# A decode block of attention and feed-forward: 549 matrix products in place of 693

## The chip, the core and the metric

The kernel runs on one core of a Trainium2 chip. The metric is the device time of one execution in microseconds (us). The kernel before takes 236.25 us, the median of three runs (236.07 to 236.47). Everything is fp32. Instructions run on five engines, each in its own program order: PE (matrix products; PEld is its weight loads), DVE (vector), ACT (scalar), POOL and SP, which here only issues the transfers from device memory. Engines wait for one another through semaphores.

## The reference, cut to what matters

One token for each of two batch entries passes an attention block over the last 4096 keys of a cache, and then a feed-forward block:

```python
mod = (silu(c) @ w_mod).reshape(2, 6, 1, 512)          # sa, ca, ga, sb, cb, gb
h = layernorm(x) * (1 + ca) + sa
q = (h @ wq)                                            # 32 heads of 128, 8 key/value heads
p = softmax(q k^T * 128**-0.5)                          # over the last W = 4096 keys
x = x + ga * ((p v) @ wo)
h = layernorm(x) * (1 + cb) + sb
x = x + gb * (silu(h @ w1) @ w2)                        # 512 -> 1792 -> 512
```

The cache slices are 4 MB for each key/value head, batch entry and side (keys or values), sixteen heads and entries in all: 67 MB. With the weights it is 97.5 MB, and every byte of it is used once.

## The kernel before, in words

**Storage.** One SBUF buffer, `store`, has three slots of 64 KB per partition. Each slot holds either a whole cache piece (four key/value heads of one batch entry, keys or values, 8.4 MB) or weights. At the start slot 1 holds `w_mod` and small early tiles, slot 2 `wq`. The pieces then take the slots in turn in the order k0, k1, v0, k2, v1, k3, v2, v3 (`order`, slot `i % 3`), and after them `wo` goes to slot 2, and `w1` and `w2` to slot 0. All these transfers are issued by SP in this order, on one queue; SP waits before each until the slot's last reader is done. A transfer that waits holds back every later one. `fetch` at the end of each step of the loop only records them; what a transfer waits for are the readers of its slot: k2 the products of `turn(0)`, v1 those of `turn(1)`, k3 those of `values(0)`, v2 those of `turn(2)`, v3 those of `values(1)`, `wo` those of `turn(3)`, `w1` those of `values(2)`.

**Order.** There is no scheduler. `Flow.record` notes each operation with the earlier ones whose regions it overlaps, and `emit` writes the instructions of each engine in exactly the order of the program text, with a wait for each such operation on another engine. So the text of the loop sets what stands behind what on PE and on ACT. In a profile nearly all instructions have line L117, in `emit`, and are told apart by their tiles.

**A step of the loop**, t = 0 to 3, has four parts:

- `scores(t)`: eight DVE transposes of 128 x 2048 keys in place, and after each one four products (one for each key/value head, 16 rows of the result, 512 columns) into `bank_a`. Then the maximum, which passes through two small products (`sel`, `negscale`) and becomes a bias, and one `Exp` on ACT, which writes the probabilities into the first 1024 columns of the key slot and their sums into `rowsum`.
- `turn(t)`: one DVE transpose of these 1024 columns and 16 products with `sel` into `tp` (bank C), each with 128 columns: four positions n of a key within a group, by four key/value heads a.
- `spread(t)`: four ACT copies from `tp` into `ptb`, each with another mask of `par`, so that `ptb` has 16 columns (four key/value heads by four query heads) for each of 128 keys of a partition.
- `values(t)`: 64 products. Product i takes the 32 columns of `ptb` of two keys as weights and 256 columns of the value slot (two keys by 128) and adds into 32 rows of `o_ps`, rows 32 * (i % 4). Then ACT copies `o_ps` out (`ob`, into the slot's first columns), and two products with `pick` add up the two keys and the four row groups into `o_all`.

The text of the loop before:

```python
for t in range(NP):
    scores(t)
    if t > 1:
        values(t - 1)
    turn(t)
    if t == 1:
        values(0)
    spread(t)
    fetch(2 * t + 4)
values(NP - 1)
```

**After the loop.** `o_all` is divided by the sums on DVE, meanwhile PE has six products of idle work (`fill`, 512 columns with 128 columns of weights, results unused). Then the product with `wo`: 24 rows wide (`product`, 512 columns, four row groups by `q % 4`), copied out by ACT as `wide`; eight rows narrow (`narrow`: four products of 128 columns, one for each row group), and `wide` added by four products with `id4`. Then the second layer norm with small DVE operations, the product with `w1` in two halves (`hp[0]`, `hp[1]`, 16 products of 224 columns each), silu of each half, and the product with `w2`: 14 rows, all narrow, into `y`. The first seven rows need the first half's silu, the other seven the second half's. Two DVE operations and a transfer to device memory end the kernel.

Of the kernel before, what the change touches and what calls it, by code (L numbers as in the profile page):

```python
# [5 lines left out]
AF = mybir.ActivationFunctionType  # L6
ALU = mybir.AluOpType
# [6 lines left out]
U = 4  # L14
# [121 lines left out]
def adaln_block(nc, x, k_cache, v_cache, wq, wo, w1, w2, c, w_mod, out):  # L136
# [54 lines left out]
    def const(shape, name):  # L191
        return buf(name, *shape)
# [33 lines left out]
    def summed(shape, name, pattern, axis=AX.X, **sizes):  # L226
# [26 lines left out]
        ident.rearrange("p (u n i) -> p n i u", u=U, n=4),  # L253
    )
    par = summed([P, U], "par", "p (y u) -> p u y", u=U)

    pick = const([P, 2, U * G, 4], "pick")
    dve.tensor_reduce(
        pick[:, :, :, 0],
        ident.rearrange("p (c n w) -> p n w c", n=2, w=U * G),  # L260
        axis=AX.X,
# [9 lines left out]
    dve.memset(eps_t, EPS)  # L271
    mrow = const([1, P], "mrow")
    pool.memset(mrow, 0.0)
    qbd = const([P, 2, 4, B, 4, 16], "qbd")
# [117 lines left out]


    o_all = bank("O")[:, : B * DH].rearrange("p (b d) -> p b d", b=B)

    def scores(t):
        hh, b = seq[t]
        kv = kt[t].rearrange("p (n j r) -> p n j r", n=NK, j=4)
        for f in range(2):
            for j in range(4):  # L400
# [3 lines left out]
                for u in range(U):  # L404
# [6 lines left out]
                    )  # L411
        mx = buf(f"mx{t}", P, 1)
        dve.tensor_reduce(mx, bank_a, axis=AX.X, op=ALU.max)
# [13 lines left out]
        pe.matmul(bp[:, 0:1], mrow, negscale, start=True, stop=True)  # L427
        bias = buf(f"bias{t}", P, 1)
        act.copy(bias, bp[:, 0:1])
# [6 lines left out]
    def turn(t):  # L436
        pr = kt[t][:, :1024]
        dve.transpose(pr, pr)
        xp = pr.rearrange("p (f k w) -> p f k w", f=2, w=32)
        for n in range(4):  # L440
            for a in range(4):
                pe.matmul(
                    tp[32 * a : 32 * a + 32].rearrange(
                        "p (f k n g) -> p f k n g", f=2, n=4, g=G
                    )[:, :, :, n],
                    sel[:, 32 * n : 32 * n + 32],
                    xp[:, :, :, G * a : G * a + G],
                    start=True,
                    stop=True,
                    skip_group_check=True,  # L450
                )

    def spread(t):
# [5 lines left out]

    def values(t):  # L460
        hh, b = seq[t]
        o_ps = bank("D")
        for i in range(64):
            c_ = i % 4
            pe.matmul(
                o_ps[32 * c_ : 32 * c_ + 32, :256],
                ptb[:, 2 * i : 2 * i + 2, :].rearrange("p n w -> p (n w)"),
                vt[t][:, 256 * i : 256 * i + 256],
                start=(i < 4),
                stop=(i >= 60),  # L470
            )
        ob = vt[t][:, :256].rearrange("p (n d) -> p n d", n=2)
        act.copy(ob.rearrange("p n d -> p (n d)"), o_ps[:, :256])
        for n in range(2):
            pe.matmul(
                o_all[64 * hh : 64 * hh + 64, b],
                pick[:, n].rearrange("p w i -> p (w i)"),
                ob[:, n],
                start=(n == 0),
                stop=(n == 1),  # L480
                skip_group_check=True,
            )
# [18 lines left out]
    for t in range(NP):  # L501
        scores(t)

        if t > 1:
            values(t - 1)
        turn(t)
        if t == 1:
            values(0)
        spread(t)
        fetch(2 * t + 4)  # L510
    values(NP - 1)

# [70 lines left out]
    ao = bank("A")[:, :P]  # L583
    for i in range(6):
        fill(512)
# [50 lines left out]
    for h in range(2):  # L636
# [12 lines left out]
        dve.tensor_mul(uT[:, ts, 0:32:16], z[:, ts, :], sg)  # L649
    y = bank("D")[:, :P]  # L650
    for tt in range(T2):
        narrow(y, uT[:, tt, :], w2t[tt], tt == 0, tt == T2 - 1)
    yo = later(P)
# [30 lines left out]
```

## Time and profile before

| What | Value |
|---|---|
| median of three runs | 236.25 us (236.07 to 236.47) |
| the profiled execution's own time | 236.48 us |
| its span, from the first to the last instruction | 234.9 us |
| PE busy, products | 152.5 us, 1386 records (each fp32 product is two) |
| DVE busy | 103.4 us, 126 instructions |
| ACT busy | 26.6 us, 49 instructions |
| bytes moved, mean rate | 97.72 MB, 416 GB/s |

The profile is of one execution, and its times count from its first instruction. A row of a timeline gives the start and the duration in us, the engine, the operation, the tiles written and read with their shapes, the count, and in brackets how long the engine sat idle before it and what released it. A row of a table of windows gives the stretch, its length, each engine's busy time and count, the clock that PE was granted (1.00 is full, 0.50 half), the mean share of the 16 transfer engines that was busy, and GB/s; these shares are rough in short windows, since one packet is up to 64 KB. `SPq` is the issue of a transfer; the time from issue to landing is listed by the page.

### The profile page before, as it was taken

What the parts mean: (1) busy time and instruction counts of PE and PEld (TensorE: products, weight loads), DVE (VectorE), ACT (ScalarE), POOL (GpSimd) and SP (SyncE); (2) the same over time, 40 slices, a digit from 0 to 9 for tenths busy, and PEclk for the clock granted to TensorE, in tenths of its full rate; (3) what the DMA queues carried; (4) which work ended last, traced back from release to release, by engine and by line L of the source; (5) the groups of instructions that cost most, each with busy time, mean ns of one, the idle gap of its engine ahead of it and who ended that gap; (6) DMA issues with size and microseconds to landing.
All of it is one profiled execution on the core that took longest, in us unless ns stands there. A gap on an engine that the chain in (4) does not pass through costs nothing.

```text
span 234.9 us, 3022 instructions
## 1 busy us (share of the span) xinstructions
PE 152.5 (65%) x1386; PEld 49.3 (21%) x1386; DVE 103.4 (44%) x126; ACT 26.6 (11%) x49; POOL 6.6 (3%) x23
## 2 busy tenths in 40 slices
PE   0003906920699479965989969329979609998695
PEld 0002201210000020004510025200005405534254
DVE  5014130130999299942199840069962100200332
ACT  2003010010000240002050020500002220003200
POOL 5000000000000000000000000000000300000000
PEclk9999975875699859997999979956999967999769
DMA  7998998989899898989999999999999999999990
GB/s 268 444 528 368 435 457 357 527 357 526 368 446 446 368 505 379 513 379 424 449 391 483 402 480 391 416 457 413 449 435 457 393 427 418 421 406 435 414 370 33
DMA packets 2496, 97.72 MB, mean 416 GB/s; under 512 B 284, under 2 KB 308, under 8 KB 564
## 3 DMA queue, kind: packets, MB, share of 16 engines
q1 hardware_dynamic: 2460, 97.52, 96.7%
q8 instruction: 11, 0.18, 0.3%
q10 hardware_dynamic: 24, 0.01, 0.0%
q14 instruction: 1, 0.01, 0.0%
HBM read 97.53 MB, written 0.00 MB: 415 GB/s over the span
## 4 chain that ended last, share of the span: by engine, by line
DMA 46%; DVE 28%; PE 18%; another core or an unknown queue 3%; ACT 2%; issue 1%; SPq 0%; POOL 0%
DVE store L117 26%; DMA store<-in_A_wq_dram 15%; DMA store<-in_A_k_cache_dram 15%; DMA store<-in_B_w_dram 15%; PE bankD L117 11%; PE bankA L117 4%; PE bankC L117 2%; DVE mx L117 2%; ACT store L117 2%; PE bankB L117 1%; PE bankO L117 1%; SPq L117 0%; DVE qbd L117 0%; DVE mg L117 0%
## 5 line engine op out<-in xcount | busy, mean ns | idle before, releaser
L117 DVE STREAM_TRANSPOSE store<-store 128x2048 f32<-128x2048 f32 (+2 forms) x40 | 77.1, 1984 | 36.5 <-DMA store<-in_A_k_cache_dram 28.7
L117 PE MATMUL bankA<-store,qbd 128*16 128x512 f32 x256 | 64.7, 1081 | 23.0 <-DVE store L117 21.7
L117 PE MATMUL bankD<-store,ptb 128*32 128x256 f32 x512 | 31.6, 410 | 7.2 <-DMA store<-in_A_v_cache_dram 7.2
L117 PE MATMUL bankD<-store 128*32 128x512 f32 (+1 forms) x256 | 22.3, 502 | 8.8 <-DMA store<-in_A_wq_dram 8.3
L117 PE MATMUL bankB<-store 128*32 128x256 f32 (+3 forms) x72 | 7.8, 504 | 21.9 <-DVE store L117 21.9
L117 PEld LDWEIGHTS bankD<-store,ptb 128*32 128x32 f32 x512 | 17.3, 119 | 20.2 <-issue 10.7
L117 PEld LDWEIGHTS bankA<-store,qbd 128*16 128x16 f32 x256 | 4.3, 97 | 77.1 <-DVE store L117 77.1
L117 PEld LDWEIGHTS bankD<-store 128*32 128x32 f32 x256 | 8.2, 119 | 22.8 <-issue 21.5
L117 ACT ACTIVATE ptb<-bankC,par 128x512 f32<-128x512 f32 x16 | 11.0, 688 | 7.3 <-PE bankC L117 6.9
L117 ACT COPY bias<-bankB 128x1 f32<-128x1 f32 x4 | 0.6, 159 | 90.1 <-PE bankB L117 90.1
L117 PE MATMUL bankC<-store,sel 128*32 128x128 f32 x128 | 6.0, 348 | 5.5 <-DVE store L117 5.5
L117 PEld LDWEIGHTS bankB<-store 128*32 128x32 f32 (+1 forms) x72 | 4.2, 166 | 25.0 <-DVE store L117 22.6
L117 PE MATMUL bankC<-qbd,store 128*128 128x512 f32 (+1 forms) x18 | 9.0, 640 | 0.0
L117 DVE STREAM_TRANSPOSE store<-bankA 128x128 f32<-128x128 f32 (+1 forms) x2 | 0.7, 367 | 18.1 <-PE bankA L117 18.1
L117 DVE TENSOR_REDUCE mx<-bankA 128x1 f32<-128x1024 f32 x4 | 4.9, 1225 | 8.5 <-PE bankA L117 8.5
L117 DVE RECIPROCAL store<-bankB 128x2 f32<-128x2 f32 x1 | 0.2, 171 | 17.7 <-PE bankB L117 17.7
L117 ACT COPY store<-bankD 128x256 f32<-128x256 f32 (+1 forms) x6 | 2.5, 412 | 47.8 <-PE bankD L117 47.8
L117 DVE STREAM_TRANSPOSE store<-bankD 128x512 f32<-128x512 f32 x2 | 1.4, 719 | 12.1 <-PE bankD L117 12.1
L117 PE MATMUL bankA<-store 128*32 128x128 f32 (+1 forms) x96 | 5.2, 376 | 1.7 <-DMA store<-in_B_w_dram 0.9
L117 POOL MEMSET store<- 128x128 f32 (+2 forms) x7 | 2.4, 350 | 135.5 <-PE bankD L117 134.9
L117 PEld LDWEIGHTS bankC<-store,sel 128*32 128x32 f32 x128 | 4.4, 139 | 6.2 <-DVE store L117 5.7
L117 ACT ACT_TABLE_LOAD x4 | 5.1, 1283 | 2.8 <-DVE id L117 2.8
(76 smaller groups left out, 51.8 us busy)
## 6 DMA issues: line engine op xcount, KB each, us to landing
store<-in_w_mod_dram SPq DMA_DIRECT2D x1, 6144.0 KB, 17.3
store<-in_A_wo_dram SPq DMA_DIRECT2D x1, 6144.0 KB, 21.6
store<-in_B_w_dram SPq DMA_DIRECT2D x1, 3584.0 KB, 35.6
store<-in_A_wo_dram SPq DMA_DIRECT2D x1, 2048.0 KB, 27.7
store<-in_B_w_dram SPq DMA_DIRECT2D x1, 2048.0 KB, 40.1
store<-in_B_w_dram SPq DMA_DIRECT2D x1, 1024.0 KB, 42.0
store<-in_B_w_dram SPq DMA_DIRECT2D x2, 256.0 KB, 42.2
store<-in_A_k_cache_dram SPq DMA_DIRECT2D x4, 33.5
```

The costliest lines, as they stand in the source:

```text
L117: ins = getattr(eng, method)(*args, **kw)
```

## The change

Four things change, and some small tiles with them.

1. `turn` no longer makes 16 products with `sel`. Four masked copies of the transposed probabilities (512 elements a partition each, mask `key[:, n]`, two on DVE and two on ACT) are written to columns 1024 to 3071 of the key slot (`zp`), and four products of 512 columns with a new 32-column matrix `gather`, one for each head a, do the rest.
2. `values` has a parameter `wide`: the first `wide` keys go four to a product (64 columns of `ptb`, 512 columns of values, into 64 rows of `o_ps`), the others two to a product as before. It is 64 of 128 keys for t = 0, 2 and 3, all 128 for t = 1. The copy out of `o_ps` has 512 columns for 256, and four products with `pick` follow for two.
3. In the loop's step t = 2, `values(1)` now stands behind `turn(2)`; before, it stood ahead of it. `values(2)` keeps its place ahead of `turn(3)`.
4. The first eight rows of `w2` go wide (eight products of 512 columns for 32 of 128), are copied out by ACT into `wide` and added by four products with `id4`, behind rows 8 to 11 and ahead of rows 12 and 13. Of the six products of idle work ahead of `wo`, two are left.

The small tiles: `key` and `gather` are made at the start (two more DVE reductions), `pick` is twice as large, `mx` and `bias` are one tile each for all steps, and `mrow` lies in the key slot, where POOL clears it in each step.

```diff
+    key = summed([P, 4], "key", "p (u n i) -> p n u i", axis=AX.XY, u=U, n=4)
+    gather = const([P, 32], "gather")
+    dve.tensor_reduce(
+        gather.rearrange("p (i u) -> p i u", u=U),
+        ident.rearrange("p (u n i) -> p i u n", u=U, n=4),
+        axis=AX.X,
+        op=ALU.add,
...
-    pick = const([P, 2, U * G, 4], "pick")
+    pick = const([P, 4, U * G, 4], "pick")
...
-        ident.rearrange("p (c n w) -> p n w c", n=2, w=U * G),
+        ident.rearrange("p (c n w) -> p n w c", n=4, w=U * G),
...
+    mx, bias = const([P, 1], "mx"), const([P, 1], "bias")
...
-        mx = buf(f"mx{t}", P, 1)
+        mrow = kt[t][0:1, 3072:3200]
+        pool.memset(mrow, 0.0)
...
         xp = pr.rearrange("p (f k w) -> p f k w", f=2, w=32)
+        zp = kt[t][:, 1024:3072].rearrange("p (f k n w) -> p f k n w", f=2, n=4, w=16)
         for n in range(4):
-            for a in range(4):
-                pe.matmul(
-                    tp[32 * a : 32 * a + 32].rearrange(
-                        "p (f k n g) -> p f k n g", f=2, n=4, g=G
-                    )[:, :, :, n],
-                    sel[:, 32 * n : 32 * n + 32],
-                    xp[:, :, :, G * a : G * a + G],
-                    start=True,
-                    stop=True,
-                    skip_group_check=True,
+            if n < 2:
+                dve.tensor_scalar(
+                    zp[:, :, :, n], xp[:, :, :, :16], key[:, n : n + 1], None, op0=ALU.mult
                 )
+            else:
+                act.activation(
+                    zp[:, :, :, n], xp[:, :, :, :16], AF.Copy, scale=key[:, n : n + 1]
+                )
+        for a in range(4):
+            pe.matmul(
+                tp[32 * a : 32 * a + 32],
+                gather,
+                zp.rearrange("p f k n w -> p (f k n) w")[:, :, G * a : G * a + G],
+                start=True,
+                stop=True,
+            )
...
-    def values(t):
+    def values(t, wide):
+
         hh, b = seq[t]
         o_ps = bank("D")
-        for i in range(64):
-            c_ = i % 4
+        n0 = 0
+        while n0 < NK:
+            n = 4 if n0 < wide else 2
+            c = n0 // n % (8 // n)
+            r, d0 = 16 * n * c, n0 % 4 * DH
             pe.matmul(
-                o_ps[32 * c_ : 32 * c_ + 32, :256],
-                ptb[:, 2 * i : 2 * i + 2, :].rearrange("p n w -> p (n w)"),
-                vt[t][:, 256 * i : 256 * i + 256],
-                start=(i < 4),
-                stop=(i >= 60),
+                o_ps[r : r + 16 * n, d0 : d0 + n * DH],
+                ptb[:, n0 : n0 + n, :].rearrange("p n w -> p (n w)"),
+                vt[t][:, DH * n0 : DH * (n0 + n)],
+                start=(n0 < 8),
+                stop=(n0 + 8 >= NK),
+                skip_group_check=True,
             )
-        ob = vt[t][:, :256].rearrange("p (n d) -> p n d", n=2)
-        act.copy(ob.rearrange("p n d -> p (n d)"), o_ps[:, :256])
-        for n in range(2):
+            n0 += n
+        ob = vt[t][:, :512].rearrange("p (n d) -> p n d", n=4)
+        act.copy(ob.rearrange("p n d -> p (n d)"), o_ps)
+        for n in range(4):
             pe.matmul(
                 o_all[64 * hh : 64 * hh + 64, b],
                 pick[:, n].rearrange("p w i -> p (w i)"),
                 ob[:, n],
                 start=(n == 0),
-                stop=(n == 1),
+                stop=(n == 3),
                 skip_group_check=True,
...
-        if t > 1:
-            values(t - 1)
+        if t == 3:
+            values(2, 64)
         turn(t)
         if t == 1:
-            values(0)
+            values(0, 64)
+        if t == 2:
+            values(1, NK)
         spread(t)
         fetch(2 * t + 4)
-    values(NP - 1)
+    values(NP - 1, 64)
...
-    for i in range(6):
+    for i in range(2):
         fill(512)
...
-    y = bank("D")[:, :P]
-    for tt in range(T2):
-        narrow(y, uT[:, tt, :], w2t[tt], tt == 0, tt == T2 - 1)
+    y = bank("A")[:, :P]
+    acc = bank("D")
+    for tt in range(8):
+        product(acc, uT[:, tt, :], w2t[tt], tt % 4, D, tt < 4, tt >= 4)
+    act.copy(wide, acc)
+    for tt in range(8, T2 - 2):
+        narrow(y, uT[:, tt, :], w2t[tt], tt == 8, False)
+    narrow(y, id4, wide, False, False)
+    for tt in range(T2 - 2, T2):
+        narrow(y, uT[:, tt, :], w2t[tt], False, tt == T2 - 1)
```

Three places show how the instructions move. The first is PE in step t = 2, from its score products (into bank A) on; bank D with `ptb` is `values(1)`, bank O its sum over keys, bank C `turn(2)`. Shapes are rows by columns of the result. A minus is the order before, a plus the order now.

```order
 L117 MATMUL bankA<-store,qbd 16x512 x32
 L117 MATMUL bankB<-sel,mx 1x128
-L117 MATMUL bankB<-negscale,mrow 128x1
-L117 MATMUL bankD<-store,ptb 32x256 x64
-L117 MATMUL bankO<-store,pick 64x128 x2
-L117 MATMUL bankC<-store,sel 32x32x4 x16
+L117 MATMUL bankB<-negscale,store 128x1
+L117 MATMUL bankC<-store,gather 32x512 x4
+L117 MATMUL bankD<-store,ptb 64x512 x32
+L117 MATMUL bankO<-store,pick 64x128 x4
```

Before, `values(1)` ran while ACT and DVE made and transposed the probabilities of step 2, and `turn(2)` followed it. Now PE has `turn(2)` next after the two small products, and `values(1)` behind it, directly ahead of the score products of step 3.

The second is ACT in step t = 3, from the copy of the bias to the last copy out of `o_ps`:

```order
 L117 COPY bias<-bankB 128x1
 L117 ACTIVATE store,rowsum<-bankA,bias 128x1024
-L117 COPY store<-bankD 128x256
+L117 COPY store<-bankD 128x512
+L117 ACTIVATE store<-store,key 128x32x16 x2
 L117 ACTIVATE ptb<-bankC,par 128x128x4 x4
-L117 COPY store<-bankD 128x256
-L117 COPY store<-bankD 128x512
+L117 COPY store<-bankD 128x512 x2
 L117 ACT_TABLE_LOAD
```

The first copy from bank D is that of `values(2)`. The two masked copies of `turn(3)` stand behind it on ACT, and the products of `turn(3)` need them.

The third is the end of PE's program, the two halves of the product with `w1` (bank A, bank B) and the product with `w2`:

```order
 L117 MATMUL bankA<-store 32x224 x16
 L117 MATMUL bankB<-store 32x224 x16
-L117 MATMUL bankD<-store 32x128 x56
+L117 MATMUL bankD<-store 32x512 x8
+L117 MATMUL bankA<-store 32x128 x16
+L117 MATMUL bankA<-store,id 32x128 x4
+L117 MATMUL bankA<-store 32x128 x8
```

Seven of the eight wide products need the first half alone; the eighth and all that follows it need the second half too.

More of the change, by code (lines that the diff above doesn't have):

```diff
@@ L271, in adaln_block @@
     dve.memset(eps_t, EPS)
-    mrow = const([1, P], "mrow")
-    pool.memset(mrow, 0.0)
     qbd = const([P, 2, 4, B, 4, 16], "qbd")
@@ L427, in scores @@
         pe.matmul(bp[:, 0:1], mrow, negscale, start=True, stop=True)
-        bias = buf(f"bias{t}", P, 1)
         act.copy(bias, bp[:, 0:1])
@@ L439, in turn @@
         xp = pr.rearrange("p (f k w) -> p f k w", f=2, w=32)
+        zp = kt[t][:, 1024:3072].rearrange("p (f k n w) -> p f k n w", f=2, n=4, w=16)
         for n in range(4):
-            for a in range(4):
-                pe.matmul(
-                    tp[32 * a : 32 * a + 32].rearrange(
-                        "p (f k n g) -> p f k n g", f=2, n=4, g=G
-                    )[:, :, :, n],
-                    sel[:, 32 * n : 32 * n + 32],
-                    xp[:, :, :, G * a : G * a + G],
-                    start=True,
-                    stop=True,
-                    skip_group_check=True,
-                )
+            if n < 2:
+                dve.tensor_scalar(
+                    zp[:, :, :, n], xp[:, :, :, :16], key[:, n : n + 1], None, op0=ALU.mult
+                )
+            else:
[9 more added lines that the diff above has]
+                stop=True,
+            )
     def spread(t):
```

## The prediction, written before the changed kernel was run

> **What bounds the kernel now.** I read the page first, then the waits, then the timeline of the transfer queue beside that of PE.
>
> ```profile
> PE 152.5 (65%) x1386; PEld 49.3 (21%) x1386; DVE 103.4 (44%) x126; ACT 26.6 (11%) x49; POOL 6.6 (3%) x23
> DMA packets 2496, 97.72 MB, mean 416 GB/s; under 512 B 284, under 2 KB 308, under 8 KB 564
> q1 hardware_dynamic: 2460, 97.52, 96.7%
> q8 instruction: 11, 0.18, 0.3%
> ...
> store<-in_A_wo_dram SPq DMA_DIRECT2D x1, 2048.0 KB, 27.7
> ```
>
> The transfers are the bound: the queue is busy for 96.7% of the span, and PE only for 65%. So compute costs nothing as long as SP finds the next slot free before the transfer in flight has landed. How much room there is, the last cache pieces show:
>
> ```profile
> 0.74 0.39 SPq L117 DMA_DIRECT2D store<-in_w_mod_dram  x1
> 149.55 1.18 SPq L117 DMA_DIRECT2D store<-in_A_v_cache_dram  x2
> 155.02 17.66 DVE L117 STREAM_TRANSPOSE store<-store 128x2048 f32<-128x2048 f32 x8 [13.53 <-DMA store<-in_A_k_cache_dram]
> 186.67 0.81 SPq L117 DMA_DIRECT2D store<-in_A_wo_dram  x2
> 193.83 6.43 PE L117 MATMUL bankD<-store,ptb 128*32 128x256 f32 x92 [7.22 <-DMA store<-in_A_v_cache_dram]
> ...
> 1.50:2.00 0.50, 0.00 (x0) 0.00 (x0) 0.47 (x2) 0.00 (x0) 0.00 (x0) 1.00 4.06 1180
> ```
>
> k3 lands at 155.0, and v2 and v3 were issued at 149.55. v3 lands at 193.8, and `wo` was issued at 186.67, when `turn(3)` freed its slot: 7.1 us ahead. The first transfer was issued at 0.74 and its bytes moved from the half microsecond after 1.5 on, so an issue needs about 1.0 us. **The room is therefore 6.1 us for `turn(3)`**; after that the transfers stop. PE waits 7.22 us for v3.
>
> **PE's price of the new products.** A product is two records.
>
> ```profile
> 177.29 7.11 PE L117 MATMUL bankD<-store,ptb 128*32 128x256 f32 x128
> 203.33 5.42 PE L117 MATMUL bankC<-qbd,store 128*128 128x512 f32 x12
> 208.68 5.36 PE L117 MATMUL bankD<-store 128*32 128x512 f32 x48
> 202.69 0.32 PE L117 MATMUL bankO<-store,pick 128*64 128x128 f32 x1 [0.49 <-ACT store L117]
> 202.70 0.28 PE L117 MATMUL bankB<-rowsum,store 128*64 128x2 f32 x2
> 202.85 0.49 PE L117 MATMUL bankO<-store,pick 128*64 128x128 f32 x3
> 138.71 8.62 PE L117 MATMUL bankD<-store,ptb 128*32 128x256 f32 x128
> ...
> 138.70:142.00 3.30, 3.30 (x37) 0.53 0.82 357
> ```
>
> Six full-width products of 512 columns take 5.42 us, of which about 0.25 is the tail of the last: 0.86 each. Twenty-four products of 32 rows and 512 columns take 5.36: 0.86 for each round of four, so four row groups run side by side, and a round lasts by its columns alone. Sixteen rounds of 256 columns take 7.11, or 0.43 each. A product of 64 rows fills two row groups, and the 64-row products of `rowsum` (lower half) begin at 202.70 beside those of `pick` (upper half, 202.69), ahead of the latter's next ones at 202.85: two halves run side by side. So eight keys, which took one round of 256 columns (0.43), now take one of 512 (0.86). **`values` goes from 7.1 to 10.5 us where half is wide (+3.4), and to 13.9 where all is (+6.8).** Fewer products, but more columns per key. The bounds: as cheap as now (7.1), or no two halves side by side (17.3 and 27.5). `values(1)` took 8.62, with a granted clock of 0.53 in its first 3.3 us: such a start costs 1.5.
>
> The transfers' own term: 549 products are 2196 instructions of PE for 2772 (the page's 1386 + 1386). 0.18 MB of instructions came in 11 packets, about 252 instructions each, so nine remain. Such a packet delays data on one of the 16 transfer engines: the second piece of `wo` (2.1 MB, 5.0 us at 416 GB/s) landed 27.7 us after 187.1, at 214.8, though the first (21.6 us after its issue) was there at 208.3; 1.5 us are lost. I take 0 to 1.5 us earlier landings at the end, worth something only if the transfers set the end.
>
> **`turn`.** Removed: 16 products of 128 columns, four abreast, so as many columns as one round of 512. Added: one such round, 0.86 + 0.2, so the 1.08 us below stay. New on the path between the transpose and the products are the masked copies.
>
> ```profile
> 185.53 1.08 PE L117 MATMUL bankC<-store,sel 128*32 128x128 f32 x32
> 186.68 2.85 ACT L117 ACTIVATE ptb<-bankC,par 128x512 f32<-128x512 f32 x4 [1.78 <-PE bankC L117]
> ...
> L117 ACT ACTIVATE store<-store 128x14 f32<-128x14 f32 x2 | 0.4, 214 | 8.3 <-DVE store L117 8.3
> L117 DVE TENSOR_SCALAR store<-store 128x128 f32<-128x128 f32 x2 | 0.5, 228 | 0.5 <-ACT store L117 0.5
> ```
>
> ACT does 512 elements with a mask from PSUM in 0.71 (four in 2.85); from SBUF no row has 512, and 14 elements take 0.21. Two copies are between 0.43 and 1.43; I take 1.3, near the row of the same size. DVE's two lie beside them: between 0.46 (two of 128 elements) and 1.8 (four times that); I take 1.0. They also push back the transposes of the next keys by 1.0, which counts once, in step 1, where DVE has no wait ahead of them.
>
> **The backlog of scores.** This decides how far PE can catch up.
>
> ```profile
> 134.03 1.98 PE L117 MATMUL bankA<-store,qbd 128*16 128x512 f32 x8 [0.21 <-DVE store L117]
> ...
> 134.80:134.90 0.10, 0.10 (x4) 1.00 3.04 1311
> 134.90:135.00 0.10, 0.10 (x8) 1.00 0.00 0
> ...
> 135.10:135.20 0.10, 0.10 (x8) 1.00 1.52 655
> 135.20:135.30 0.10, 0.10 (x4) 1.00 0.00 0
> ```
>
> A group of four score products takes 1.98 us. Its second records begin near 134.9 while the first are still listed until 135.2. Groups that follow without a wait can overlap likewise: about 1.75 each, with 1.98 as the other bound. DVE sends a group every 2.2 us (17.66 / 8), so eight groups catch up 3.6 us at most.
>
> **The walk.**
>
> ```profile
> 110.16 7.54 PE L117 MATMUL bankD<-store,ptb 128*32 128x256 f32 x128
> 118.21 0.65 PE L117 MATMUL bankO<-store,pick 128*64 128x128 f32 x4 [0.50 <-ACT store L117]
> 136.08 1.23 DVE L117 TENSOR_REDUCE mx<-bankA 128x1 f32<-128x1024 f32 x1 [2.10 <-PE bankA L117]
> 140.25 1.25 DVE L117 STREAM_TRANSPOSE store<-store 128x1024 f32<-128x1024 f32 x1 [2.02 <-ACT store L117]
> 174.78 1.23 DVE L117 TENSOR_REDUCE mx<-bankA 128x1 f32<-128x1024 f32 x1 [2.10 <-PE bankA L117]
> ...
> L117 ACT COPY store<-bankD 128x512 f32<-128x512 f32 x1 | 0.6, 587 | 11.5 <-PE bankD L117 11.5
> ```
>
> - Step 1: `turn(1)` ended at 110.4; with +1.0 (DVE) and +1.3 it ends at 112.7. `values(0)` took 7.54 and takes 10.9 plus about 0.3 more at half clock: 123.9. Copy 0.6 and four `pick` products 1.1 (two: 0.65): 125.6 for 118.9.
> - `scores(2)` waited for keys before; now PE is late: 125.6 + 8 x 1.75 + 0.2 = 139.8, for 136.0. From the maximum's start to the end of the transpose 5.4 us (136.08 to 141.50): 145.2; copies 1.3; four products at half clock 1.9: 148.5. v2 can go out then, for 149.55: no harm.
> - `values(1)` now stands here: 148.5 + 13.9 + 1.5 = 163.9, copy and `pick` 1.75: 165.7. v3 goes out while v2 is in flight: no harm. But `scores(3)` stands behind it: its keys are there from 155.0, and its first group, at 157.4 before, starts at 165.7. It ends at 165.7 + 14.2 = 179.9, for 174.8.
> - Step 3: 2.5 us later (174.78 to 177.29) `values(2)` starts, 182.4, + 10.5 + 1.2 for part of a start at half clock = 194.1. Behind it on ACT stand its copy (0.6) and then the masked copies (1.3), then four products (1.1): **`turn(3)` ends at 197.1, for 186.6.**
>
> `wo` is issued 10.5 us later with 6.1 us of room: **the queue is empty for 4.4 us**, from 193.8 to about 198.2. In a sentence apart, the Trainium skill, page "DMA: Bandwidth & Descriptors" (Specifications), gives about 0.6 us to the first byte from SP; the trace shows 1.0, and by the page the gap would be an estimated 4.0.
>
> **After the loop.**
>
> ```profile
> 214.83 1.95 PE L117 MATMUL bankA<-store 128*32 128x128 f32 x64 [0.80 <-DMA store<-in_A_wo_dram]
> 223.22 3.21 PE L117 MATMUL bankA<-store 128*32 128x224 f32 x32 [0.94 <-DMA store<-in_B_w_dram]
> 230.67 1.74 PE L117 MATMUL bankD<-store 128*32 128x128 f32 x56 [0.28 <-DVE store L117]
> ...
> 231.50:232.00 0.50, 0.50 (x28) 0.50 (x20) 0.00 (x0) 0.00 (x0) 0.00 (x0) 1.00 0.13 33
> ```
>
> `spread(3)` (2.9) ends at 200.0, and `values(3)` starts there for 193.8: +6.2. It is 3.4 longer, copy and `pick` 0.65, four fills fewer give back 4 x 0.86 = 3.4: +6.8 at the products with `wo`. PE waited 0.80 for the second part of `wo` and 0.94 for `w1`; both waits go, which leaves +5.1 at `w1`'s products, 228.3. `w1` itself lands 12.1 MB after the queue's restart, 29 us at 416 GB/s, at 227.2, so PE is the later one.
>
> The product with `w2`: seven rows of the second half took 1.74, 0.25 a row. Now the eighth wide row takes 0.86, rows 8 to 11, the `id4` products and rows 12 and 13 seven times 0.25: 2.6 in all, or 2.2 if three of the row groups run ahead beside it. I take +0.7; nothing below zero, since the last rows of `w2` moved until 231.5 to 232.0 before.
>
> At nothing: `key`, `gather` and the larger `pick` in DVE's 11 us ahead of `x`; POOL's clears of `mrow` (0.2 each), which wait for half of the scores and are done long before `mg`.
>
> Sum: 236.48 + 5.1 + 0.7 = 242.3 against the profiled execution, which lay 0.2 above the median: **242.0 us.**
>
> **The rivals.**
>
> *PE has the room, and the change is faster.* If eight keys in a wide round cost no more than in a narrow one, `turn(3)` ends near 188 (177.3 + 7.1, then copy, masks and products, 3.0, and some lateness), inside 192.7, the queue never stops, and the end is the old one with landings up to 1.5 earlier and +0.7: 235.5. The point is `turn(3)` at 192.7. For it: the waits of 13.5 and 7.2 us for the cache are real slack. Against it: 0.86 for 512 columns, alone or four abreast, in two rows. The Trainium skill, page "TensorE: Matmul & The Clock Gate" (Part 3, What overlaps and what doesn't), has products begin and end strictly in program order. By that rule the two records of one product would part it from its neighbours, a narrow product would cost 0.21, a wide one 0.43, and the change would cost `values` nothing; but then 64 narrow ones would need 13.7 us, and 7.11 is measured. Chance 0.10.
>
> *A small gap, no change.* All starts find the full clock (-1.5, -1.2), the copies cost 0.5 (-2.4 over three steps): `turn(3)` ends at 192; PE's lateness of 1.8 at the products with `wo` goes into its two waits, and +0.7 stands against landings up to 1.5 earlier, half of which I take: 236.2. Chance 0.07.
>
> *Two halves do not run side by side.* `values` takes 17.3 or 27.5; `scores(2)` is 6.8 later, `values(1)` 13.6, `values(2)` 6.8: `turn(3)` near 224, `values(3)` 6.8 longer too, the end near 275. Only the `rowsum` rows speak against it. Chance 0.06.
>
> *The forecast*, a gap and a late PE, 237.2 to 246: 0.77.
>
> **How the numbers follow.** Within the forecast the scores at 1.98 add twice 1.8 (245.6); cheap copies take off 2.4, full clock 2.7 (236.9). The range 237.0 to 246.0 leaves out the two outer rivals and most of the small gap. A measurement tells 0.2%, 0.5 us, from no change. Faster: 0.09 of the first rival and 0.01 of the small gap, 0.10; within: 0.01 + 0.06 + 0.01 = 0.08; slower 0.82.
>
> **What would show it.** In the changed profile: bank D's group of 64 rows at 0.86 per two products; `scores(3)` without waits for DVE; the issue of `wo` near 197, after v3's landing; in the slices, a lower share of the transfers behind 193; the wait of PE for v3 gone; nine instruction packets. I am wrong if `wo` is issued before 192.7, or if the score groups in a backlog come much faster than 1.75.

## The result: slower by 3.7%, and the profile after

The changed kernel takes 244.70 us (median of six runs, 244.23 to 245.87) for 236.16 of the kernel before (six runs): a ratio of 1.0369, with a 95% interval of 1.0341 to 1.0397. The prediction was 242.0, with 237.0 to 246.0 as its range, and slower as the likeliest case. The profiled execution took 245.87 us, the longest of the six, with a span of 244.5; the numbers below are its. One execution of the kernels below, of 245.51 us with the masked copies apart, is over 1.5% above the fastest of its kernel, counts as slow and stands in no median and no ratio.

The page of the changed kernel first: the busy share of the 16 transfer engines in 40 equal slices of the span, then two queues with packets, MB and share.

```profile
DMA  7999998989798989899799989899989409989991
...
q1 hardware_dynamic: 2460, 97.52, 93.3%
q8 instruction: 8, 0.13, 0.2%
```

The queue of the data was at 96.7% before. The slices with 4 and 0 are a hole, 190 to 202 us into the span. SP's issues of v1, k3, v2 with v3, and `wo` (start, duration; a long duration is a wait ahead of the last of them):

```profile
113.88 0.53 SPq L117 DMA_DIRECT2D store<-in_A_v_cache_dram  x1
128.14 0.54 SPq L117 DMA_DIRECT2D store<-in_A_k_cache_dram  x1
152.92 17.31 SPq L117 DMA_DIRECT2D store<-in_A_v_cache_dram  x2
...
201.02 0.81 SPq L117 DMA_DIRECT2D store<-in_A_wo_dram  x2
```

`wo` went out at 201.0, for 186.7 before and 197.1 predicted. In the trace's record of landings (each transfer lands on 16 engines, each at its own time) v3 landed from 194.1 to 196.0, so the hole begins there. PE's timeline shows why `wo` was late: `values(0)`, `scores(2)`, `values(1)`, `scores(3)`, `values(2)`, `turn(3)`, `values(3)` and the product with `w1`:

```profile
113.75 12.56 PE L117 MATMUL bankD<-store,ptb 128*64 128x512 f32 x96
128.04 14.92 PE L117 MATMUL bankA<-store,qbd 128*16 128x512 f32 x64
152.79 15.10 PE L117 MATMUL bankD<-store,ptb 128*64 128x512 f32 x64
169.59 14.92 PE L117 MATMUL bankA<-store,qbd 128*16 128x512 f32 x64
187.09 10.68 PE L117 MATMUL bankD<-store,ptb 128*64 128x512 f32 x96
199.90 1.06 PE L117 MATMUL bankC<-store,gather 128*32 128x512 f32 x8 [0.29 <-ACT store L117]
203.93 13.55 PE L117 MATMUL bankD<-store,ptb 128*64 128x512 f32 x96 [2.97 <-ACT ptb L117]
232.93 1.74 PE L117 MATMUL bankA<-store 128*32 128x224 f32 x32
```

None of the first six waits for a transfer any more: the 7.22 us that PE waited for v3 are gone, and so are the waits for DVE inside the scores. `values` of half wide keys takes 10.68 where the clock is full (7.11 before), the all-wide one 15.10. At the end PE still meets a transfer, `w1`. The row of its weight loads shows it:

```profile
232.93 1.30 PEld L117 LDWEIGHTS bankA<-store 128*32 128x32 f32 x32 [0.90 <-DMA store<-in_B_w_dram]
```

Most of these 0.90 us are not a wait for `w1`: two idle products (230.90 to 232.86) stand ahead of it in the program, and behind them the weight loads sit idle for 0.76 us even where `w1` has long landed (a row of a later run shows it below). PE itself was kept for about 0.1 us.

From 232.93 to the span's end it is 11.6 us, for 11.7 before (223.22 to 234.9). So the whole loss was made ahead of `w1`.

The windows of the same trace (stretch and length; busy time of PE, PEld, DVE, ACT, POOL; clock; transfer share; GB/s), one early in `values(0)`, shown for its clock, two in the hole, one early in `values(3)`, again for the clock:

```profile
117.00:118.00 1.00, 1.00 (x6) 0.38 (x4) 1.00 (x1) 0.00 (x0) 0.00 (x0) 0.70 0.00 0
...
196.00:197.00 1.00, 1.00 (x28) 0.58 (x20) 0.00 (x0) 0.00 (x0) 0.00 (x0) 1.00 0.00 0
...
200.00:201.00 1.00, 0.96 (x8) 0.05 (x8) 0.00 (x0) 0.00 (x0) 0.13 (x1) 1.00 0.00 0
...
204.00:206.00 2.00, 2.00 (x6) 0.70 (x8) 0.00 (x0) 0.00 (x0) 0.00 (x0) 0.50 0.91 393
```

No byte moves from v3's last landing at 196.0 to the issue of `wo` at 201.0, while PE is at work, or ACT on PE's results: the transfers wait for them. `values(3)`, like `values(0)`, starts at half clock, and that is why it takes 13.55 and not 10.68: in the trace the clock is half from 202.9 to 209.8, which covers 5.9 us of `values(3)`, and half of these is 2.9.

Last, the masked copies of `turn(1)`, DVE's two and ACT's two:

```profile
109.32 1.01 DVE L117 TENSOR_SCALAR store<-store,key 128x512 f32<-128x512 f32 x2
...
110.36 1.47 ACT L117 ACTIVATE store<-store,key 128x512 f32<-128x512 f32 x2 [2.36 <-DVE store L117]
```

They run one after the other. The four masks write interleaved columns, `Flow.record` compares regions by their outer bounds and sees an overlap, so ACT waits for DVE: 2.5 us in all, where the prediction had them side by side in 1.3.

### The profile page after: what moved, and what is told of

Its sections match the earlier page's. It is cut to its first block, busy times and chain, and to the rows that moved or that the text cites. A ratio compares the mean times of both kernels' runs of the same rounds, so it can differ in the third digit from the quotient of the medians.

```text
span 244.5 us, 2471 instructions
## 1 busy us (share of the span) xinstructions
PE 165.5 (68%) x1098; PEld 49.1 (20%) x1098; DVE 107.7 (44%) x136; ACT 33.6 (14%) x58; POOL 7.4 (3%) x26
## 4 chain that ended last, share of the span: by engine, by line
PE 39%; DMA 30%; DVE 21%; ACT 4%; another core or an unknown queue 3%; issue 1%; SPq 1%; POOL 0%
PE bankD L117 20%; DVE store L117 18%; DMA store<-in_B_w_dram 15%; DMA store<-in_A_wq_dram 15%; PE bankA L117 15%; ACT store L117 4%; PE bankC L117 3%; DVE mx L117 2%; PE bankB L117 1%; PE bankO L117 1%; SPq L117 1%; DVE qbd L117 0%; DVE mg L117 0%; POOL store L117 0%
## 5 line engine op out<-in xcount | busy, mean ns | idle before, releaser
L117 PE MATMUL bankA<-store,qbd 128*16 128x512 f32 x256 | 61.5, 1090 | 12.3 <-DVE store L117 11.8
L117 PE MATMUL bankD<-store,ptb 128*32 128x256 f32 (+1 forms) x352 | 51.9, 514 | 3.0 <-ACT ptb L117 3.0
L117 PE MATMUL bankD<-store 128*32 128x512 f32 x160 | 20.5, 661 | 10.1 <-DMA store<-in_A_wq_dram 8.4
L117 PEld LDWEIGHTS bankD<-store,ptb 128*32 128x32 f32 (+1 forms) x352 | 18.3, 131 | 38.4 <-issue 30.9
L117 PEld LDWEIGHTS bankA<-store,qbd 128*16 128x16 f32 x256 | 8.4, 107 | 59.9 <-DVE store L117 39.4
L117 PE MATMUL bankC<-store,gather 128*32 128x512 f32 x32 | 6.9, 947 | 16.2 <-ACT store L117 16.2
L117 ACT COPY store<-bankD 128x512 f32<-128x512 f32 (+1 forms) x7 | 3.9, 559 | 64.9 <-PE bankD L117 64.9
L117 POOL MEMSET store<- 128x128 f32 (+3 forms) x11 | 3.2, 295 | 148.2 <-PE bankA L117 127.3
L117 ACT ACTIVATE store<-store,key 128x512 f32<-128x512 f32 x8 | 5.8, 721 | 7.2 <-DVE store L117 7.1
L117 PE MATMUL bankO<-store,pick 128*64 128x128 f32 x32 | 4.3, 279 | 2.9 <-ACT store L117 2.9
```

The costliest lines, as they stand in the source:

```text
L117: ins = getattr(eng, method)(*args, **kw)
```

## The experiments

The theory: wide products double PE's time per key; PE falls behind; what frees a slot of the store (a step of PE's) comes later than the landing it should precede; the queue runs empty. The rivals: the new turn, the moved `values(1)`, or the end of the kernel cost the time. All ratios are to the kernel before, measured beside each.

| Kernel | us, median | ratio (95%) |
|---|---|---|
| changed kernel | 244.70 | 1.0369 (1.0341 to 1.0397) |
| changed, all keys narrow | 236.99 | 1.0050 (1.0019 to 1.0080) |
| before, with wide values only | 243.96 | 1.0334 (1.0307 to 1.0362) |
| before, with the new turn only | 236.97 | 1.0041 (1.0024 to 1.0059) |
| before, with w2's wide rows only | 236.25 | 1.0014 (1.0005 to 1.0023) |
| changed, masked copies apart | 242.11 | 1.0291 (1.0218 to 1.0365) |
| changed, values(1) half wide | 241.42 | 1.0231 (1.0210 to 1.0251) |
| both of the last two | 239.87 | 1.0171 (1.0154 to 1.0188) |
| changed, values(2) behind turn(3) | 249.36 | 1.0543 (1.0504 to 1.0583) |
| placed anew, half wide | 238.69 | 1.0099 (1.0061 to 1.0137) |
| placed anew, values(3) narrow | 235.44 | 0.9980 (0.9965 to 0.9995) |
| placed anew, all narrow | 235.96 | 0.9997 (0.9985 to 1.0009) |
| placed anew, values(3) narrow, padded | 236.00 | 0.9998 (0.9989 to 1.0007) |

### One part alone, or taken back

**All keys narrow**, the rest of the change left in:

```diff
-            values(2, 64)
+            values(2, 0)
...
-            values(0, 64)
+            values(0, 0)
...
-            values(1, NK)
+            values(1, 0)
...
-    values(NP - 1, 64)
+    values(NP - 1, 0)
```

> The changed kernel with every key two to a product (values' parameter 0 in all four steps), the rest of the change left in: new turn, values(1) behind turn(2), four pick products, w2's first rows wide, two fills. Theory (a wide round costs twice the PE time per key, PE is late, turn(3) issues wo after v3 has landed, the queue runs empty): values are 7.1 to 8.6 us again, each step is 3.4 to 6.8 us earlier, wo goes out near 190 to 192, close to v3's landing or ahead of it, and the time is 235.5 to 237.5. Rival, the new turn with its serial copies or the moved values(1) is what costs: the time stays at 240 or more. Rival, the end of the kernel (w2's wide rows, fewer fills) costs: 238 to 240.

236.99, inside the theory's numbers, 7.7 us below the changed kernel. `wo` goes out ahead of v3's landing (from 193.7):

```profile
179.27 8.80 PE L117 MATMUL bankD<-store,ptb 128*32 128x256 f32 x128
...
191.33 0.81 SPq L117 DMA_DIRECT2D store<-in_A_wo_dram  x2
```

The new turn, the moved `values(1)`, four `pick` products, two idle products and the wide rows of `w2` are all still there, so together they cost, on balance, the 1.0 us that is left.

**The wide values alone**, in the kernel before, at the old places (here, and in the next run, with the small tiles as in the changed kernel):

```diff
-            values(t - 1)
+            values(t - 1, NK if t == 2 else 64)
...
-            values(0)
+            values(0, 64)
...
-    values(NP - 1)
+    values(NP - 1, 64)
```

> The kernel before with the wide values alone (64, 128, 64, 64 keys four to a product, four pick products), at their old places, with the old turn, the old w2 and six fills. Theory: turn(3) ends near 195 to 197 for 186.6, v1 and v2 go out about as early as before, v3 later because values(1) is 6.8 us longer, the queue is empty before wo, and the time is 240 to 244.5. Rivals, the new turn or w2's rows cost it: 235.5 to 237.5 here.

243.96: the time as expected, nearly the whole loss from this one part. The all-wide `values(1)`, which starts at full clock here, takes 13.95, as predicted (13.9). But the hole is not in the place expected:

```profile
141.00 13.95 PE L117 MATMUL bankD<-store,ptb 128*64 128x512 f32 x64
...
157.80 1.49 SPq L117 DMA_DIRECT2D store<-in_A_v_cache_dram  x2
...
180.26 12.70 PE L117 MATMUL bankD<-store,ptb 128*64 128x512 f32 x96 [3.15 <-DMA store<-in_A_v_cache_dram]
```

At its old place the all-wide `values(1)` stands ahead of `turn(2)`, which frees the slot for v2. v2 went out at 157.8, after k3 had landed (152.9 to 154.8), and the queue was empty there, not before `wo`. Moving `values(1)` behind `turn(2)`, as the change does, takes the hole away from v2 and leaves it to `wo`; the time is about the same.

**The new turn alone**, in the kernel before:

```diff
-                pe.matmul(
-                    tp[32 * a : 32 * a + 32].rearrange(
...
+            if n < 2:
+                dve.tensor_scalar(
+                    zp[:, :, :, n], xp[:, :, :, :16], key[:, n : n + 1], None, op0=ALU.mult
...
+                act.activation(
+                    zp[:, :, :, n], xp[:, :, :, :16], AF.Copy, scale=key[:, n : n + 1]
```

> The kernel before with the new turn alone (masked copies and four products with gather). Theory: the copies, in series, cost 2.5 us a step, which lies in the room of 6.1 us before wo; v1 is issued near 113 and lands up to 2 us later as in the changed kernel, so 236 to 238. Rival, the new turn is the cause of the loss: 241 or more.

236.97, as the theory had it: slower by 1 us. In the profiled execution, the longest of the ten (237.85), v1 goes out 3.0 us later than before (110.45), and lands at 135.1 on the first engine for 133.6:

```profile
113.49 0.54 SPq L117 DMA_DIRECT2D store<-in_A_v_cache_dram  x1
```

**The wide rows of `w2` alone**, in the kernel before:

```diff
+    for tt in range(8):
+        product(acc, uT[:, tt, :], w2t[tt], tt % 4, D, tt < 4, tt >= 4)
+    act.copy(wide, acc)
+    for tt in range(8, T2 - 2):
+        narrow(y, uT[:, tt, :], w2t[tt], tt == 8, False)
+    narrow(y, id4, wide, False, False)
...
```

> The kernel before with the first eight rows of w2 wide, nothing else (six fills stay). Theory: +0 to +0.9 us (the eighth wide row, 0.86, and the tail of narrow rows behind the second half's silu), 236.2 to 237.1. Rival, the end costs most of the loss: 239 or more.

236.25 for 236.01: +0.24 us. The end of the kernel is no cause.

### How much each us of PE weighs

**Masked copies in rows apart**, so that ACT doesn't wait for DVE:

```diff
-        zp = kt[t][:, 1024:3072].rearrange("p (f k n w) -> p f k n w", f=2, n=4, w=16)
+        zp = kt[t][:, 1024:3072].rearrange("p (n f k w) -> p n f k w", n=4, f=2, w=16)
...
-                zp.rearrange("p f k n w -> p (f k n) w")[:, :, G * a : G * a + G],
+                zp.rearrange("p n f k w -> p (f k) n w")[:, :, :, G * a : G * a + G],
```

> The changed kernel, but each masked copy has rows of its own in the key slot (mask n outermost), so that ACT's two copies no longer wait for DVE's two. Theory: turn(1) and turn(2) end 1.0 earlier each (v1 issued near 112.8 for 113.9, v2 near 150.9), turn(3) 2 to 3 us earlier (wo near 198 to 199), v1's own gap shrinks from 2 us to about 1, and the time is 241.8 to 243.2 for 244.7. Rival, the copies' wait lies in slack: 244.2 or more. The products read their 128 pieces of 4 columns in another stride; if that were dearer, bank C's eight records would be longer than 1.06.

Inconclusive by its size: three runs fell at 241.7, 242.1 and 245.2, and the interval of the ratio holds the expected gain as well as almost none. The profiled execution is the one of 245.51, so its trace can't tell what the edit gains. It does show that the edit does what it should: the copies ran side by side, ACT's ending at 110.4 for 111.8, and v1 went out 1.5 earlier.

```profile
109.04 1.33 ACT L117 ACTIVATE store<-store,key 128x512 f32<-128x512 f32 x2 [1.31 <-DVE store L117]
...
112.42 0.53 SPq L117 DMA_DIRECT2D store<-in_A_v_cache_dram  x1
```

**`values(1)` half wide**:

```diff
-            values(1, NK)
+            values(1, 64)
```

> The changed kernel with values(1) half wide (64 of 128 keys) as in the other steps. Theory: PE is late from values(1) on by its whole length, so scores(3), turn(3), wo's issue and the end come 3.4 to 3.8 us earlier: wo near 197.4, time 240.8 to 241.8. Rival, the time is lost elsewhere (v1's gap, the end): within 1 us of the changed kernel, 243.7 or more.

241.42: 3.3 us less, for 3.5 us less of PE's time (`values(1)` takes 11.60 for 15.10). `wo` goes out 4.2 earlier in the profiled executions, which lie 4.6 apart (241.26 and 245.87):

```profile
196.81 0.81 SPq L117 DMA_DIRECT2D store<-in_A_wo_dram  x2
```

**Both edits together**:

> The changed kernel with both single edits that had an answer: masked copies in rows apart, and values(1) half wide. Theory: the two add, since both lie on the one path of PE to turn(3). The half-wide one alone came to 241.4 with wo issued at 196.8; the copies apart bring v1 out 1.5 us earlier (its gap of 2 us shrinks to 0.7) and turn(1) and turn(2) 1.2 each: wo near 194 to 195, 1 to 2 us behind v3's landing near 192.7, time 238.7 to 240.3. Rival, the copies' wait lies in slack, and the two short runs of the copies apart had another cause: 241.0 or more.

239.87; the two add up (1.5 us on top of the 3.3), which tells the copies' share better than their own run: they lie on PE's path, not in slack. `wo` is out at 193.46, in a profiled execution that is the shortest of the five (238.14).

### Is it the hole, or PE itself?

**`values(2)` behind `turn(3)`**:

```diff
-        if t == 3:
-            values(2, 64)
         turn(t)
...
+        if t == 3:
+            values(2, 64)
         spread(t)
```

> The changed kernel with values(2) behind turn(3) instead of ahead of it. turn(3) no longer waits for 10.7 us of products, so wo is issued near 190 to 191 for 201.0, ahead of v3's landing at 194 to 196, and most of the queue's gap of 8.7 us goes. But spread(3) stands behind values(2): values(3) starts near 206 for 203.9 and PE is 2 us later than in the changed kernel at the products with wo and with w1. If the transfers alone set the end (PE waited 0.90 us for w1), 238 to 241; if PE is next in line, as the prediction had it, 244.5 to 249. I expect the second, since 0.90 us is all that PE has to spare there.

249.36, the second of the two cases, just above its upper end. The rows are the issue of `wo`, `values(3)`, and the product with `w1`, with PE's weight loads for it:

```profile
192.70 0.81 SPq L117 DMA_DIRECT2D store<-in_A_wo_dram  x2
...
207.42 12.38 PE L117 MATMUL bankD<-store,ptb 128*64 128x512 f32 x96 [1.66 <-ACT ptb L117]
...
235.11 1.74 PE L117 MATMUL bankA<-store 128*32 128x224 f32 x32
...
235.11 1.30 PEld L117 LDWEIGHTS bankA<-store 128*32 128x32 f32 x32 [0.76 <-issue]
```

The hole is nearly gone, the last byte of `w2` landed at 233.0 for 241.5, and the kernel is slower, because PE alone now needs until 235.1 to reach `w1`, without any wait for it: `w1` had landed by 224.3. The weight loads are idle for 0.76 all the same, so of the 0.90 in the changed kernel only about 0.1 was the transfer's, and the expectation above, which took all of it as PE's to spare, was too generous. So in the changed kernel two things are late by nearly the same amount, the transfers and PE; to fill the hole alone would gain about 0.1 us at `w1`, and half a us behind it (from `w1` to the span's end it is 11.1 us here, and 11.6 there, where PE waits for the last rows of `w2` too). This trace is of the shortest of the four executions (247.49): it accounts for the 1.6 us by which that one is longer than the changed kernel's profiled one, and not for the 4.7 between the medians, which stay unexplained.

### Wide where there is room

**Placed anew**: the old turn at t = 1, masked copies apart and at t = 0 all on ACT, half of the keys wide in each step, `values(2)` behind `turn(3)`, no idle products ahead of `wo`.

```diff
+        if t == 1:
+            for n in range(4):
+                for a in range(4):
+                    pe.matmul(
...
-            if n < 2:
+            if n < 2 and t > 0:
...
-        if t == 3:
-            values(2, 64)
         turn(t)
...
-            values(1, NK)
+            values(1, 64)
+        if t == 3:
+            values(2, 64)
...
-    for i in range(2):
-        fill(512)
```

> Half of the keys wide in all four steps, but with the work placed so that the theory sees no transfer wait: the old turn at t = 1 (v1 out near 110.5), the masked copies of t = 0 all on ACT, those of t = 2 and 3 in rows apart, values(1) behind turn(2) and values(2) behind turn(3), no idle products ahead of wo. Theory: v2 out near 149, v3 near 161, wo near 185, all ahead of the landing before them; values(3) starts near 199 and ends near 210, and PE meets w1 at 221 to 223, with its landing. Time 235.0 to 237.0, as before. Rival, a wide round costs the transfers something of its own (or PE's lateness passes through anyway): 239 or more.

238.69: missed by 1.7 us at the least. No issue was late, and the last byte of `w2` landed at 230.3, earlier than before (231.8). But PE was:

```profile
213.29 7.05 PE L117 MATMUL bankD<-store 128*32 128x512 f32 x48 [1.55 <-DVE store L117]
...
226.60 1.74 PE L117 MATMUL bankA<-store 128*32 128x224 f32 x32
```

The products with `wo` took 7.05 for 5.36. Without idle products PE stood for 1.55 us ahead of them, and then its clock was halved:

```profile
215.00:217.00 2.00, 2.00 (x12) 0.44 (x8) 0.00 (x0) 0.00 (x0) 0.00 (x0) 0.50 0.93 401
```

I had counted the idle products as pure cost; there they fill a wait. PE reached `w1` at 226.6, not at 221 to 223. The clock is 1.7 of this; the rest is in the expectation, which left 11 to 13 us from the end of `values(3)`, rightly put near 210, to `w1`, where the changed kernel takes 15.4 at full clock (217.5 to 232.9). So `values(3)` half wide was more than PE had room for.

**The same with `values(3)` narrow and two idle products back**:

```diff
-    values(NP - 1, 64)
+    values(NP - 1, 0)
...
+    for i in range(2):
+        fill(512)
```

> The kernel placed as in the one before it in this study (old turn at t = 1, masked copies apart and at t = 0 on ACT, values(1) behind turn(2), values(2) behind turn(3)), half of the keys wide for t = 0, 1 and 2, but values(3) narrow, and two idle products ahead of wo again. There PE reached w1's products at 226.6 and set the end; values(3) is 3.4 shorter, and the idle products lie in a wait of 1.55 and keep the clock (1.7): w1's products near 221.6 to 222, where w1 lands (219.6 to 221.7 there, 219.7 to 223.2 in the kernel before). Theory: neither the queue nor PE is late, 2372 instead of 2772 instructions of PE: 234.6 to 236.0, faster than the kernel before by 0.2 to 1.5 us. Rival, wide values cost something beside PE time and queue gaps: 237.5 or more.

235.44, as expected, and 0.2% faster than the kernel before (0.9980, interval 0.9965 to 0.9995): the fastest of all kernels here. 192 keys are wide in it (three steps of 64), for 320 in the changed kernel.

```profile
209.76 5.36 PE L117 MATMUL bankD<-store 128*32 128x512 f32 x48
...
222.22 2.52 PE L117 MATMUL bankA<-store 128*32 128x224 f32 x32
```

**The same with all keys narrow**:

```diff
-            values(0, 64)
+            values(0, 0)
...
-            values(1, 64)
+            values(1, 0)
...
-            values(2, 64)
+            values(2, 0)
```

> The same with all keys narrow (2564 instructions of PE). Theory: 235.0 to 236.3, within 0.7 us of the half-wide one, since PE has room there; if wide values still cost something where PE has room, this one is faster by 1 us or more; if fewer instruction packets bring something, it is slower by 0.2 to 0.8.

235.96. Here PE waits for the first part of `wo` (2.85 us) and for `w1` (1.06 us), so it has time to spare, and wide products cost nothing where it has. They may bring a little. The wait for `wo` is longer than the two idle products, and behind it the products with `wo` take 7.05 again:

```profile
208.44 7.05 PE L117 MATMUL bankD<-store 128*32 128x512 f32 x48 [2.85 <-DMA store<-in_A_wo_dram]
...
222.87 1.74 PE L117 MATMUL bankA<-store 128*32 128x224 f32 x32 [1.06 <-DMA store<-in_B_w_dram]
```

**The half-wide one, padded** with products of one element at the start, so that PE has as many instructions as in the kernel before:

```diff
+    for i in range(100):
+        pe.matmul(bank("C")[0:1, 0:1], negscale, negscale, start=True, stop=True)
```

> The half-wide one (values(3) narrow) with 100 idle products of one element at the very start, while PE waits for w_mod (2772 instructions of PE again, as in the kernel before; nothing else differs). If the gain over the kernel before comes from fewer instruction packets among the transfers, one or two packets more come before w1 has landed, the slowest of the 16 transfer engines lags by up to 1.5 us more, and this is 0.3 to 1.5 us slower than without the pad. If the packets mean nothing, it is the same within 0.3 us.

236.00, 0.56 above the one without. The page of the padded kernel counts 11 instruction packets, that of the other 9:

```profile
q8 instruction: 11, 0.18, 0.3%
```

```profile
q8 instruction: 9, 0.15, 0.2%
```

In the profiled executions the last part of `w2` lands over 3.0 us from the first of the 16 engines to the last (228.3 to 231.3), for 2.2 (228.1 to 230.3) without the pad, and 3.4 in the kernel before. This is what fewer packets would do. But the difference of the two means, 0.44 us, has a standard error of 0.21 over 12 runs each: it points that way and doesn't settle it.

## Why the prediction was right, and where its sizes were off

**Right: the mechanism.** That a wide round costs twice a narrow one: predicted 10.5 and, with a start at half clock, 15.4, measured 10.68 and 15.10. That 64-row halves run side by side, that the scores turn into a backlog, that `turn(3)` and with it `wo` come after v3's landing, that the queue is empty there. With all keys narrow the loss is 1.0 us, with wide ones alone it is 7.95. The rival by which PE has the room falls with the 10.68, the one by which halves don't pair too, and the small gap with the size of the hole.

**Off: the time, 242.0 for 244.7.** Against the profiled execution it is 242.3 for 245.87, 3.6 us. PE's start on `w1` came 4.6 later than predicted (232.93 for 228.3); the tail gave 0.8 back (predicted +0.7, measured -0.1) and what lies around the span 0.2. Two of the misses below ran the other way, 1.0 at `values(2)` and the 0.8 of the tail, so that the total came nearer than its terms: that part was luck. The steps that failed:

- *The masked copies* (step 1 and step 3 of the walk, 1.3 side by side): 2.5 in series, 1.2 more in each of the steps t = 1 and 2. The region rule that makes ACT wait is in the kernel before too; the prediction left it out.
- *`values(0)`*: 11.2 predicted, 12.56 measured. It ran at half clock until near 117.6, longer than the 0.3 us that I took. `values(2)` started at full clock instead and was 1.0 cheaper than predicted, `values(3)` at half and 1.7 dearer (13.55 for 11.8).
- *The backlog of scores*: 1.75 a group predicted, 14.92 / 8 = 1.87 measured, the same within 1% wherever eight groups ran without a wait (14.71 to 14.94). In two steps that is 1.4 us.
- These, with the all-wide `values(1)` 0.3 cheaper, add up to `wo` at 201.0 for 197.1, 3.9 us.
- *The restart of the queue* (1.0, from the very first transfer): too small. From an issue into an empty queue to the first engine's landing of `wo`'s first part there are 16.4 us (201.02 to 217.44); behind a busy queue v3's and its first landings were 14.5 apart (191.72 to 206.26 before). So a restart costs about 1.9. The hole is 217.44 - 194.05 - 14.54 = 8.9 us by the first landings (8.6 by the last ones), predicted 4.4.
- *The room* (6.1 us for `turn(3)`), the same term seen from the other end: it was counted to v3's last landing, less 1.0. With the new turn alone `wo` went out 2.3 us ahead of v3's first landing, with all keys narrow 2.4, and its own came 0.7 and 0.8 later than behind a busy queue; with the wide values alone it went out 3.0 ahead and was not late. Counted from 191.7, the first landing before, that leaves 2.0 to 2.7 us of room. With `wo` 14.3 us late this changes the size of the hole and not what follows, since the landings then count from the issue.
- *v1* was not in the prediction at all. Its walk used the end of `turn(1)` as the start of `values(0)`, and passed over that the same end issues v1. Eight traces show the size: with the issue at 110.45 v1's first landing is at 133.6, and with issues at 112.33, 112.42, 113.49, 113.55, 113.87, 113.88 and 114.03 it comes 21.6 to 22.0 later than the issue, 134.2 to 135.8. By these two numbers an issue has to be out by about 111.7, 2.4 us ahead of the 114.1 at which k2's first engine is done; no run lies between 110.45 and 112.33. The new turn alone costs its 1.0 us there and at `wo`. In the changed kernel it costs nothing: `wo` goes out into an empty queue, and its landing counts from its own issue.
- *PE or the transfers last.* The prediction had PE at `w1` at 228.3 and its landing at 227.2. Measured, the landing was at 232.9 and PE ready about 0.1 earlier: nearly a tie, with the transfers last and not PE. The run with `values(2)` last shows it too: with the transfers out of the way PE, 2.2 us later at `w1` in the trace, is late by itself.

**The tail** was to cost 0.7: alone it costs 0.24, and in the changed kernel nothing on balance, since the first half of the product with `w1` took 1.74 for 3.21: PE came to it from work, not from a wait. **The packets**: nine predicted, eight came; the transfers did set the end there, so the 0 to 1.5 us that the prediction named lie somewhere in the 244.7 and can't be read from it; the padded pair points to about half a us.

## What to carry to other kernels

Where one engine's steps release the transfers, its busy share says nothing of its room; walk its program from release to release, and count for each issue how far ahead of the landing in flight it has to be, here between 2.4 and 3.0 us ahead of its first engine's. Fewer matrix instructions aren't less matrix time: count columns per key, and make products wide only at steps whose end nothing on the path waits for. And a hole in the queue is not the price by itself: before it is filled by reordering, see whether the engine that caused it wouldn't be the next one late.

## What the runs showed of the hardware that was not expected

- A queue must be fed before it looks empty. `wo` issued 3.0 us ahead of v3's first landing came 14.5 us behind it, as behind a busy queue; issued 2.3 and 2.4 us ahead it came 15.2 and 15.4 behind it. Issued after v3's first landing, in four traces, it took 16.4 to 16.5 us to its first landing, 1.8 to 2.0 more than 14.5. By the Trainium skill, page "DMA: Bandwidth & Descriptors" (Anatomy of one DMA), a transfer has a fixed cost of about 2.0 us, most of it between the last byte and the signal; it is stated for transfers issued by POOL. The 1.8 to 2.0 are of that size, but they don't show that cost: the 14.5 run from one landing to the next, so what follows a last byte is in both.
- Products of different row groups can start out of program order. In the placed kernel with `values(3)` narrow, PE's program has the eight wide products with `w2` (bank D, 16 records) and then the narrow ones (bank A). The timeline has them so:

```profile
226.97 2.63 PE L117 MATMUL bankD<-store 128*32 128x512 f32 x15 [0.70 <-DVE store L117]
229.03 0.64 PE L117 MATMUL bankA<-store 128*32 128x128 f32 x12
229.44 0.59 PE L117 MATMUL bankD<-store 128*32 128x512 f32 x1
```

  Twelve records of bank A begin before the last record of bank D. The Trainium skill, page "TensorE: Matmul & The Clock Gate" (Part 3, What overlaps and what doesn't), has products start and end strictly in program order; the starts in these rows differ, and they decide. It is the case of three row groups running ahead, for which the prediction had 2.2 instead of 2.6.
- The clock at a start is not a constant of the program. The same half-wide `values` took 10.68 to 13.65 us by the clock that it found. Behind the same two waits (1.34 and 0.54 us, 1.35 and 0.54) the narrow `values(2)` took 7.11 in the kernel before and 8.80, from 180.1 to 183.5 at half clock, in the changed one with all keys narrow. 1.55 us of standing still, without idle products, made the products with `wo` 1.7 us longer; two idle products in that wait kept them at 5.36 in two traces, and didn't in a third, where the wait for `wo` was longer than they are.
